# Engine orders as written-out tables in a gated linear attention and squared-relu kernel

## The chip, the cores and the metric

The kernel runs on one core of one Trainium2 chip. The metric is device time in microseconds, from the first to the last instruction of the program; of several runs the median is given.

## The reference

A recurrent linear attention with a decay per channel feeds a two-layer network with a squared relu. 4 batches, 8 heads, 768 tokens, head size 48; the network has width 384 and 2048 hidden units.

```python
def _attn_ref(q, k, v, alpha):
    state = np.zeros((B, H, D, D)); y = np.zeros_like(q)
    for t in range(S):
        state = alpha[:, :, t, :, None] * state + np.einsum('bhd,bhe->bhde', k[:, :, t], v[:, :, t])
        y[:, :, t] = np.einsum('bhd,bhde->bhe', q[:, :, t], state)
    return y

def _moe_ref(x, w_in, w_out):
    h = x @ w_in
    r = np.maximum(h, 0.0)
    g = r * r
    return g @ w_out
```

The attention's output, laid out as 3072 tokens by 384, is x. Inputs and output are float32.

## The kernel before

**Units.** The tokens are cut into 12 units (G = 12) of 256 tokens of one batch, numbered 0 to 11; units 0 to 3 are the first of their batches, 8 to 11 the last. The recurrence is computed in chunks: running sums of the logarithms of alpha give decay factors, with which q and k are scaled, so that the work inside a chunk is matmuls, and a state of 48 x 48 per head is handed from a batch's unit to its next.

**Steps of a unit g, with the names that the text uses** (a name is that of an operation handed to `Program.add`):

- loads: `lda`, `ldk`, `ldq`, `ldv` (L568), four DMAs of 384 KB into RAW, of which there are four buffers. Those of unit 2 go through GpSimd's queue, all others through SyncE's. All loads of a unit from 4 on wait until `ldq` of the unit before has landed; from unit 5 on `lda` also waits for the unit before's `ln`, `ldk` for its `ekm`, `ldq` and `ldv` for its `tr0`. The loads of unit 3 wait for the weight load `wout0`. `win0`, `win1`, `wout0`, `wout1` (L539) bring the two layers' weights in two halves each (768 KB on arrival, as bf16) through GpSimd's queue; `win0` and `win1` wait for `lda1`, and `lda2` to `ldv2`, `wout0` and `wout1` wait for `ldv1`.
- front: `pr` (product of two tokens' alphas, L675 or L677), `ln` (L678) and `lm` (L717) on ScalarE, `m1i` (running sum, a matmul, L684 and L687; units 2 and 3 also have `m1s`), `ei`, `ea`, `ec` (exponentials out of PSUM, L695 to L700), `bk` (L702 or L704), `lb` (L719), `es` (L721; in units 2 and 3 L709, followed by `aq`), then `ekm` (L751) and `eqm0`, `eqm1` (L746), which scale k and q. `vc` casts v to bf16 (L741 on GpSimd or L742 on ScalarE; L613 in unit 0). `tr0` and `tr1` (L762) transpose the scaled q and k by DMA from unit 3 on, before that on TensorE, with `et` as the copies out of PSUM (L641, L783). Unit 0's front is cut by heads, so that its names have one digit more (`ekm0_0`, `ekm1_0`, `tr01_0`).
- attention: `p` (scores, L940), `mk0` and `mk1` (the causal mask, L951), `kv` (keys by values, L811), `sa`, `sc`, `sd` (the state, L904 to L917), `y` (the output, L832 and L843; from y2 to y10 it holds the `kv` of the next unit too), `xe` (copy out of PSUM, L971), `xt` (transpose; on TensorE, L986, with the copy `xv` up to unit 3, by DMA on SyncE's queue, L992, from unit 4 on).
- network: eight steps `s1_g_u` (six matmuls each, L1042) write two PSUM banks in turn; `re` takes the relu (512 columns, L1050 on ScalarE or L1052 on VectorE); `sq` squares it, 1024 columns where u is 1, 3 or 5, and 512 where it is 6 or 7 (L1060 on VectorE, L1064 on ScalarE; the form for GpSimd stands at L1063). Two times four steps `s2_g_j_s` (four matmuls each, L1089) sum into the one bank psO, `oe_g_j` (L1097 or L1099) copies it out, and `out` (L1109) stores 384 KB. The last half tile of unit 11 is cut into two parts of 272 and 112 columns (L1012, L1017, L1019, L1020).

**What sets the order.** Each operation is added with the engines that may run it, a cost for each, a priority, and the keys that it reads and writes. `schedule` (L159) then plays the program through with these costs, with a rate for each DMA and with corrections of the priorities from the table SHIFT, and so gives every operation an engine and a place in that engine's order. `fill` (L271) puts matmuls of zeros (L1143, 512 or 256 columns) on TensorE where it expects idle time ahead of the first s1. `place` (L298) works out which semaphores each operation has to wait for, and `emit` (L348) writes each engine's instructions in that order. On the chip every engine takes its instructions strictly in that order.

TensorE's order around unit 7 and 8 before: `y8 s1_7_2 s1_7_3 m1i10 s2_7_0_0 s1_7_4`. SyncE's: `ldq9 ldv9 out5_1 lda10 ldk10 tr0_9 tr1_9 out6_1 xt8 ldq10 ldv10 lda11`. GpSimd's start: `vc0 win0 win1 sd0 lda2 ldk2 ldq2 ldv2 wout0 wout1 sd1 pr3`.

Of the kernel before, what the change touches and what calls it, by code (L numbers as in the profile page):

```python
# [2 lines left out]

# [28 lines left out]


class Program:

    HOP = 35
    PE_LATENCY = 170
    DMA_FIRST = {"sp": 1300, "act": 1300, "pool": 2000}  # L40
    PACKET = (("win", 172), ("wout", 490), ("ld", 22), ("tr", 18), ("xt", 18), ("out", 125))
    SBUF_ONLY = ("pr", "bk", "aq", "ekm", "eqm", "sq", "sb", "sd")
    BIAS = {"pool": 300}
    DMA_LAST = {"sp": 800, "act": 800, "pool": 1900}
    SWITCH = 95
# [1129 lines left out]
```

## Time and profile before

| | |
|---|---|
| runs | 175.18, 175.5, 174.51 us; median 175.18 |
| the profiled execution's span | 174.5 us |
| granted TensorE clock | 1.000 |
| first s1 matmul, last matmul, last end | 18.46, 171.91, 174.47 us |
| ScalarE: relus L1050 | 83, 596 ns each |
| VectorE: relus L1052 | 13, 687 ns each |
| VectorE: squares L1060 | 30 of 1024 columns, 712 ns; 17 of 512, 424 ns |
| ScalarE: squares L1064 | 6 of 1024 columns, 1057 ns; 7 of 512, 631 ns |
| SyncE's DMAs, 384 KB load, issue to landing | 4.2 to 5.1 us (medians) |
| GpSimd's weight loads, issue to landing | 9.9 and 15.2 us (medians) |

The page is of one execution. An engine's busy time is the union of its instructions; PE is TensorE's matmuls, PEld its weight loads, DVE VectorE, ACT ScalarE, POOL GpSimd, SP SyncE, of which only the queue (SPq) issues. In the strips of 40 digits each stands for a fortieth of the span, in tenths of it busy. A group has the line, the engine, the operation, its output and inputs with shapes, the count, then busy us and mean ns of one, then the idle time just ahead of its instructions and who ended it. A line of a timeline has the start in us, the duration, the engine, and at its end in brackets the idle time before.

### The profile page before, as it was taken

What the parts mean: (1) busy time and instruction counts of PE and PEld (TensorE: products, weight loads), DVE (VectorE), ACT (ScalarE), POOL (GpSimd) and SP (SyncE); (2) the same over time, 40 slices, a digit from 0 to 9 for tenths busy, and PEclk for the clock granted to TensorE, in tenths of its full rate; (3) what the DMA queues carried; (4) which work ended last, traced back from release to release, by engine and by line L of the source; (5) the groups of instructions that cost most, each with busy time, mean ns of one, the idle gap of its engine ahead of it and who ended that gap; (6) DMA issues with size and microseconds to landing.
All of it is one profiled execution on the core that took longest, in us unless ns stands there. A gap on an engine that the chain in (4) does not pass through costs nothing.

```text
span 174.5 us, 5094 instructions
## 1 busy us (share of the span) xinstructions
PE 169.1 (97%) x2237; PEld 130.5 (75%) x2237; DVE 121.3 (70%) x197; ACT 117.6 (67%) x211; POOL 18.8 (11%) x28
## 2 busy tenths in 40 slices
PE   7989999999999999999999999999999999999994
PEld 2556898856886697777788886778788697688773
DVE  5497799797967869866778966868849726322230
ACT  3848698868869569768768757378668564566440
POOL 3159010022102120000100000000200000000000
DMA  5999999979998999798998897999899690040022
GB/s 139 324 297 190 274 303 216 230 208 280 274 229 125 274 235 188 200 222 151 278 212 211 228 196 180 275 201 251 201 214 208 115 196 4 0 135 4 10 80 90
DMA packets 74743, 33.36 MB, mean 191 GB/s; under 512 B 71649, under 2 KB 71905, under 8 KB 74721
## 3 DMA queue, kind: packets, MB, share of 16 engines
q1 hardware_dynamic: 73184, 28.32, 71.4%
q0 software_dynamic: 1536, 4.72, 12.1%
q8 instruction: 17, 0.28, 0.7%
q14 instruction: 6, 0.04, 0.1%
HBM read 25.17 MB, written 4.72 MB: 171 GB/s over the span
## 4 chain that ended last, share of the span: by engine, by line
PE 56%; DMA 26%; ACT 6%; DVE 4%; SPq 3%; POOL 2%; issue 1%
PE psO L1089 22%; PE psWH L1042 22%; DMA raw<-in_v_dram 9%; DMA wout<-in_moe_w_out_dram 8%; DMA raw<-in_alpha_dram 5%; DMA raw<-in_q_dram 5%; SPq L568 3%; PE psO L1143 2%; POOL raw L568 2%; ACT rr L1050 2%; PE psX L843 2%; PE psX L1012 2%; ACT vbf L742 1%; PE psZ L811 1%; PE psX L832 1%; PE psX L940 1%
## 5 line engine op out<-in xcount | busy, mean ns | idle before, releaser
L1042 PE MATMUL psWH<-xt,win 128*128 128x256 bf16 x576 | 73.9, 275 | 0.5 <-ACT rr L1050 0.2
L1042 PEld LDWEIGHTS psWH<-xt,win 128*128 128x128 bf16 x576 | 65.0, 145 | 6.2 <-DVE rr L1052 1.6
L1089 PE MATMUL psO<-wout,gt 128*128 128x384 bf16 x368 | 68.9, 326 | 0.0
L1050 ACT ACTIVATE rr<-psWH 128x512 bf16<-128x512 f32 x83 | 48.9, 596 | 21.5 <-PE psWH L1042 20.0
L1089 PEld LDWEIGHTS psO<-wout,gt 128*128 128x128 bf16 x368 | 34.8, 98 | 18.3 <-DVE gt L1060 0.2
L1060 DVE TENSOR_TENSOR gt<-rr 128x1024 bf16<-128x1024 bf16 (+1 forms) x47 | 28.4, 608 | 25.1 <-ACT rr L1050 24.5
L951 DVE TENSOR_TENSOR pm<-psX,caus 128x1024 bf16<-128x1024 f32 x12 | 14.6, 1220 | 2.4 <-PE psZ L940 2.1
L951 DVE TENSOR_TENSOR pm<-psZ,caus 128x1024 bf16<-128x1024 f32 x12 | 14.6, 1216 | 1.5 <-PE psZ L940 1.4
L1097 ACT ACTIVATE osb<-psO 128x384 f32<-128x384 f32 x19 | 9.3, 489 | 6.8 <-PE psO L1089 6.3
L971 ACT ACTIVATE xbf<-psX 128x768 bf16<-128x768 f32 x12 | 9.7, 806 | 5.0 <-PE psX L832 4.1
L746 DVE TENSOR_TENSOR qks<-raw,eq 128x384 bf16<-128x384 f32 x18 | 10.3, 605 | 3.0 <-DMA raw<-in_q_dram 3.0
L1143 PE MATMUL psO<-zero 128*128 128x512 bf16 (+1 forms) x37 | 10.5, 417 | 1.3 <-DVE zero L489 1.3
L741 POOL CAST vbf<-raw 128x768 bf16<-128x768 f32 x4 | 3.7, 930 | 71.5 <-DMA raw<-in_v_dram 71.5
L1064 ACT ACTIVATE gt<-rr 128x512 bf16<-128x512 bf16 (+1 forms) x13 | 10.8, 828 | 0.4
L751 DVE TENSOR_TENSOR qks<-raw,ek 128x768 bf16<-128x768 f32 x11 | 10.7, 969 | 0.4 <-ACT ek L663 0.3
L1052 DVE TENSOR_SCALAR rr<-psWH 128x512 bf16<-128x512 f32 x13 | 8.9, 687 | 2.0 <-PE psWH L1042 1.6
L742 ACT ACTIVATE vbf<-raw 128x768 bf16<-128x768 f32 x7 | 5.9, 845 | 3.5 <-DMA raw<-in_v_dram 3.5
L717 ACT ACTIVATE la<-raw 128x384 f32<-128x384 f32 x8 | 4.2, 523 | 5.3 <-DMA raw<-in_alpha_dram 5.2
L1143 PEld LDWEIGHTS psO<-zero 128*128 128x128 bf16 x37 | 3.5, 108 | 4.6 <-issue 1.9
L906 DVE TENSOR_TENSOR smd<-psZ,sbd 128x384 bf16<-128x384 f32 x8 | 4.4, 554 | 3.4 <-PE psX L832 3.4
L675 DVE TENSOR_TENSOR prd<-raw 128x384 f32<-128x384 f32 x7 | 4.0, 569 | 2.9 <-DMA raw<-in_alpha_dram 2.9
L678 ACT ACTIVATE lab<-prd 128x384 bf16<-128x384 f32 x10 | 5.2, 520 | 1.1 <-POOL prd L677 0.6
(115 smaller groups left out, 165.9 us busy)
## 6 DMA issues: line engine op xcount, KB each, us to landing
raw<-in_alpha_dram SPq DMA_DIRECT2D x11, 384.0 KB, 4.2
raw<-in_k_dram SPq DMA_DIRECT2D x11, 384.0 KB, 5.1
raw<-in_q_dram SPq DMA_DIRECT2D x11, 384.0 KB, 4.2
raw<-in_v_dram SPq DMA_DIRECT2D x11, 384.0 KB, 4.8
...
wout<-in_moe_w_out_dram POOLq DMA_DIRECT2D x2, 768.0 KB, 15.2
...
```

What stands on the lines that cost most here:

```text
L746: add("dve", lambda e, j=j, dst=dst: e.tensor_tensor(dst, RAW[r][:, 2, :, j, :].rearrange("p (n x) d -> p n x d", x=2), EQ[la][:, j].rearr ...
L751: add("dve", lambda e, a=a, E=E: e.tensor_tensor(QKS[qs][:, a, :, :, 0:D], RAW[r][:, 1 + a].rearrange("p h j d -> p j h d"), E[la][:].rear ...
L951: add("dve", lambda e, hf=hf, psT=psT: e.tensor_tensor(PM[pm][:, hf].rearrange("p r n j t -> p (r n) (j t)"), psT[:, :, :].rearrange("p r ...
L971: add("act", lambda e: e.activation(XBF[x2][:], psX[:, :, 0:HD], AF.Copy), act_ns(2 * HD), p0 + 6100, reads=[("ps", "X", 0), ("ps", "X", 1 ...
L1042: ins = pe.matmul(psH[hb][:, i * T:(i + 1) * T], WIN[:, kk, hidden(fj)], mov, start=(kk == 0), stop=(kk == KT - 1))
L1050: add("act", lambda e, hb=hb, rr=rr: e.activation(rr, psH[hb], AF.Relu), act_ns(512), pu + 600, reads=[("ps", "H", hb)], writes=[("rr", rb ...
L1052: alts={"dve": (lambda e, hb=hb, rr=rr: e.tensor_scalar(rr, psH[hb], 0.0, None, ALU.max), dve_ns(512))})
L1060: add("dve", lambda e, dst=dst, sq=sq: e.tensor_tensor(dst, sq, sq, ALU.mult), 148 + k * 267, pu + 1200, reads=[("rr", rb, h) for h in ran ...
L1064: "act": (lambda e, dst=dst, sq=sq: e.activation(dst, sq, AF.Square), act_ns(k * 512))})
L1089: ins = pe.matmul(psS, GT[gt][:, fj, j, :], WOUT[:, fj, :], start=(fj * parts % FT == 0), stop=((fj + 1) * parts % FT == 0))
L1097: add("act", lambda e, j=j, psS=psS: e.activation(OSB[ob][:, j], psS, AF.Copy), act_ns(DM), ps_ + 700, reads=[keyS], writes=[("osb", ob, j ...
L1143: pr.fill(lambda n: lambda pe: pe.matmul(psO[:, 0:n], ZERO[:, 0:128], ZERO[:, 0:n], skip_group_check=True), ((512, 216, 420), (256, 109, 2 ...
```

## The change

`schedule`, `fill` and SHIFT go. In their place stand one table for each engine, TABLES, with the names of its operations in order (`+512` and `+256` are the matmuls of zeros), and `arrange`, which gives every operation the engine and the place that the tables say. `sequence` puts the operations of all engines into one order that respects what each depends on, which `place` used to take from the planned start times. In `add` a set `shared` notes operations that are ordered only because both read the same PSUM bank; `place` asks for no semaphore between two such on the same engine. The setup operations get names. The operations themselves, their tiles and their data stay as they are.

```diff
     def add(self, ...):
...
-        op = Op(choices, prio + self.SHIFT.get(name, 0), name)
+        op = Op(choices, prio, name)
...
             if k[0] == "ps":
                 for r in self.readers.get(k, ()):
-                    op.deps.setdefault(r, False)
+                    if r not in op.deps:
+                        op.deps[r] = False
+                        op.shared.add(r)
...
             for r in self.readers.get(k, ()):
                 if r is not op:
                     op.deps.setdefault(r, False)
+                    op.shared.discard(r)
...
+    def arrange(self, tables, make, after):
+        named = {o.name: o for o in self.ops}
...
+        for e, text in tables.items():
+            self.order[e] = []
+            for x in text.split():
+                if x[0] == "+":
+                    o = Op({e: (make(int(x[1:])), 0)}, 0, "fill")
...
+                else:
+                    o = named.pop(x)
+                o.eng = e
+                o.fn, o.cost = o.alts[e]
+                o.pos = len(self.order[e])
+                self.order[e].append(o)
...
+    def sequence(self):
+        done, seq = set(), []
+        at = {e: 0 for e in self.order}
+        while len(seq) < len(self.ops):
+            before = len(seq)
+            for e, ops in self.order.items():
+                while at[e] < len(ops) and all(d in done for d in ops[at[e]].deps):
+                    o = ops[at[e]]
+                    done.add(o)
+                    seq.append(o)
+                    at[e] += 1
...
     def place(self):
-        seq = sorted(self.ops, key=lambda o: (o.start, o.idx))
+        seq = self.sequence()
...
-                if d.sem is None and d.eng == o.eng == "pe":
+                if d.sem is None and d.eng == o.eng and (o.eng == "pe" or not raw and d in o.shared):
                     continue
...
-    pr.schedule()
-    pr.fill(lambda n: lambda pe: pe.matmul(psO[:, 0:n], ZERO[:, 0:128], ZERO[:, 0:n], skip_group_check=True),
-            ((512, 216, 420), (256, 109, 250)), min(o.start for o in pr.order["pe"] if o.name.startswith("s1_")), zero, 4600)
+    pr.arrange(TABLES, lambda n: lambda pe: pe.matmul(psO[:, 0:n], ZERO[:, 0:128], ZERO[:, 0:n], skip_group_check=True),
+               zero)
     pr.place()
     pr.emit()
```

The tables:

```diff
+TABLES = {
+    "act": """
+        table ln0_0 ln1_0 xcaus ei0_0 ei1_0 ea0_0 ea1_0 ec0_0 et00_0 ec1_0 ln1 ei1 ea1 xe0 et0_1 ec1 re0_0 xe1
+        sq0_1 ln2 re0_4 re0_6 ei2 ea2 ec2 es2 re1_1 re1_2 sq0_7 et0_2 re1_3 sq1_1 re1_4 sq1_3 re1_5 oe0_0 ln3
+        vc2 ei3 ea3 ec3 vc3 es3 re1_7 oe0_1 re1_6 lm4 xe2 ln4 sq1_7 ei4 ea4 ec4 sq1_6 re2_0 es4 re2_1 oe1_0
+        sq2_1 re2_3 lm5 ln5 ei5 ea5 vc4 re2_6 re2_7 ec5 oe1_1 es5 xe3 xv3 vc5 re3_1 re3_0 lm6 ln6 xe4 ei6 ea6
+        sq3_1 ec6 oe2_1 re3_5 sq3_5 es6 re3_6 re3_7 re4_0 re4_1 vc6 sq4_1 ln7 oe3_0 ei7 ea7 re4_5 lm7 ec7 re4_4
+        es7 re4_7 sq4_5 oe3_1 vc7 sq4_6 ln8 lm8 oe4_0 re5_3 ei8 ea8 es8 sq5_1 re5_5 re5_4 oe4_1 re6_1 re6_3 vc8
+        lm9 ln9 xe7 ei9 re6_2 re6_7 ea9 es9 sq6_5 re6_6 sq6_3 re7_1 sq6_6 ln10 re7_3 ei10 lm10 ea10 re7_2 re7_4
+        es10 oe6_1 re7_6 re7_7 sq7_6 re8_0 ln11 sq8_1 re8_3 ei11 lm11 sq8_3 re8_4 ea11 re8_7 re8_6 es11 re9_1
+        sq8_6 vc11 re9_3 oe8_0 re9_5 re9_2 sq9_5 re9_7 re9_6 sq9_7 sq9_6 oe9_1 re10_4 re10_5 sq10_7 oe10_0
+        re11_2 sq11_1 re11_4 re11_6 oe11_10 oe11_11
+    """,
+    "dve": """
+        zero zlstr zlb0 zlinc zown zqk1 zla0 zident zones zown0 zcaus1 zqk0 zcaus zown1 ekm0_0 ekm1_0 zlb1
+        eqm0_0 zla1 eqm1_0 et10_0 sa0 et01_0 et11_0 mk0_0 mk1_0 ekm1 eqm1 xv0 et1_1 zqk2 sc0 mk1_1 mk0_1 sa1
+        re0_1 re0_2 re0_3 sq0_3 re0_5 xv1 sc1 re0_7 re1_0 ekm2 aq2 eqm2 sq0_5 et1_2 sq0_6 mk1_2 mk0_2 sq1_5 sd1
+        sa2 ekm3 sc2 eqm1_3 aq3 pr4 eqm0_3 sd2 sa3 xv2 bk4 lb4 eqm1_4 ekm4 eqm0_4 re2_2 pr5 re2_4 sc3 re2_5 sd3
+        mk0_3 mk1_3 lb5 sq2_6 sq2_3 ekm5 sq2_7 sa4 eqm0_5 sc4 eqm1_5 oe2_0 mk0_4 mk1_4 pr6 re3_2 sa5 re3_3 sq3_3
+        bk6 re3_4 ekm6 lb6 sc5 eqm1_6 eqm0_6 mk0_5 sd5 mk1_5 re4_3 re4_2 xe5 sa6 sc6 lb7 ekm7 sq4_7 eqm0_7
+        eqm1_7 re4_6 mk1_6 mk0_6 re5_0 pr8 re5_1 xe6 sa7 re5_2 bk8 lb8 sc7 ekm8 eqm1_8 eqm0_8 sq5_3 re5_7 re5_6
+        sq5_6 mk1_7 mk0_7 pr9 oe5_0 re6_0 sa8 re6_5 sq6_1 bk9 ekm9 sq6_7 lb9 re6_4 eqm1_9 oe5_1 eqm0_9 mk0_8
+        pr10 re7_0 mk1_8 sq7_1 bk10 oe6_0 xe8 lb10 sa9 ekm10 sd6 eqm1_10 eqm0_10 re7_5 mk1_9 mk0_9 re8_1 sq7_5
+        sq7_7 xe9 re8_2 oe7_0 sa10 re8_5 sq8_5 bk11 lb11 oe7_1 sd7 ekm11 eqm1_11 eqm0_11 mk1_10 mk0_10 re9_0
+        xe10 sa11 sq9_1 re9_4 oe8_1 sq9_3 mk1_11 mk0_11 re10_1 re10_0 oe9_0 xe11 re10_2 re10_3 re10_6 re10_7
+        re11_0 re11_1 re11_3 oe10_1 re11_5 sq11_5 re11_7 sq11_7 sq11_6 oe11_0
+    """,
+    "pe": """
+        +512 +512 +512 +512 +512 +512 +512 +512 m10_0 m11_0 +512 +512 +512 +256 tr00_0 +512 +512 +512 +256
+        tr10_0 kv0 tr01_0 p0_0 tr11_0 +512 +512 p1_0 m11 +512 +512 +512 +256 y0 +512 +512 +512 +256 +256 tr0_1
+        xt0 +256 tr1_1 +512 +512 +512 +256 p0_1 s1_0_0 s1_0_1 kv1 s1_0_2 y1 s1_0_3 xt1 s1_0_4 s1_0_5 m1i2 s1_0_6
+        s1_0_7 s1_1_0 s1_1_1 m1s2 s1_1_2 s2_0_0_0 tr0_2 s2_0_0_1 s1_1_3 tr1_2 s1_1_4 s1_1_5 p0_2 s2_0_0_2
+        s2_0_0_3 s1_1_6 s1_1_7 m1i3 s2_0_1_0 kv2 s2_0_1_1 m1s3 s2_0_1_2 s2_0_1_3 y2 s2_1_0_0 s2_1_0_1 xt2 m1i4
+        s2_1_0_2 s1_2_0 s1_2_1 s2_1_0_3 s1_2_2 s1_2_3 s2_1_1_0 s1_2_4 s1_2_5 s2_1_1_1 m1i5 p0_3 s1_2_6 s1_2_7
+        s2_1_1_2 s2_1_1_3 y3 s2_2_0_0 s2_2_0_1 xt3 s2_2_0_2 s2_2_0_3 s1_3_1 p0_4 s1_3_0 s2_2_1_0 s2_2_1_1 s1_3_2
+        y4 s1_3_3 m1i6 s2_2_1_2 s2_2_1_3 s1_3_4 s1_3_5 s2_3_0_0 s1_3_6 s1_3_7 s2_3_0_1 p0_5 s1_4_0 s1_4_1
+        s2_3_0_2 s1_4_2 s1_4_3 s2_3_0_3 y5 m1i7 s1_4_5 s1_4_4 s2_3_1_0 s1_4_7 s2_3_1_1 s2_3_1_2 s2_3_1_3 s1_4_6
+        p0_6 s2_4_0_0 s1_5_1 s1_5_0 s2_4_0_1 s2_4_0_2 y6 s2_4_0_3 s1_5_2 s1_5_3 m1i8 s2_4_1_0 s2_4_1_1 s1_5_5
+        s2_4_1_2 s1_5_4 s2_4_1_3 p0_7 s1_5_7 s1_5_6 s2_5_0_0 s1_6_1 s2_5_0_1 s1_6_0 s1_6_3 s2_5_0_2 s2_5_0_3
+        s1_6_5 y7 m1i9 s1_6_2 s2_5_1_0 s1_6_7 s2_5_1_1 s2_5_1_2 s1_6_4 s2_5_1_3 p0_8 s1_6_6 s2_6_0_0 s1_7_1
+        s1_7_0 s2_6_0_1 s2_6_0_2 s1_7_3 m1i10 s2_6_0_3 s1_7_2 y8 s2_6_1_0 s2_6_1_1 s1_7_4 s1_7_5 s2_6_1_2
+        s2_6_1_3 s1_7_6 p0_9 s2_7_0_0 s1_7_7 s1_8_0 s2_7_0_1 s1_8_1 y9 s1_8_2 m1i11 s1_8_3 s2_7_0_2 s2_7_0_3
+        s1_8_4 s1_8_5 s2_7_1_0 s2_7_1_1 s1_8_7 s2_7_1_2 s2_7_1_3 s1_9_1 s1_8_6 s2_8_0_0 s2_8_0_1 s2_8_0_2 p0_10
+        s1_9_3 s1_9_0 s2_8_0_3 s1_9_5 y10 s2_8_1_0 s1_9_2 s2_8_1_1 s2_8_1_2 s1_9_4 s2_8_1_3 s1_9_7 s1_9_6
+        s2_9_0_0 p0_11 s2_9_0_1 s1_10_1 s1_10_0 s2_9_0_2 y11 s2_9_0_3 s1_10_3 s1_10_2 s2_9_1_0 s2_9_1_1 s2_9_1_2
+        s2_9_1_3 s1_10_4 s1_10_5 s2_10_0_0 s1_10_6 s2_10_0_1 s1_10_7 s1_11_0 s2_10_0_2 s1_11_1 s2_10_0_3 s1_11_2
+        s1_11_3 s2_10_1_0 s2_10_1_1 s2_10_1_2 s2_10_1_3 s1_11_5 s1_11_4 s2_11_0_0 s1_11_7 s1_11_6 s2_11_0_1
+        s2_11_0_2 s2_11_0_3 s2_11_1_0 s2_11_1_1
+    """,
+    "pool": """
+        scaus1 slinc slstr scaus vc0 sident win0 lda2 win1 ldk2 wout0 ldq2 vc1 wout1 ldv2 sd0 pr2 bk2 pr3 bk3
+        bk5 sq2_5 sd4 sq3_7 sq3_6 pr7 sq4_3 bk7 sq5_5 sq5_7 vc9 sq7_3 vc10 pr11 sq8_7 sq10_1 sq10_3 sq10_5
+        sq10_6 sq11_3
+    """,
+    "sp": """
+        lda0 ldv0 ldk0 ldq0 lda1 ldq1 ldv1 ldk1 lda3 ldq3 ldv3 ldk3 ldq4 lda4 ldk4 ldv4 out0_1 tr1_3 lda5 tr0_3
+        tr0_4 ldk5 tr1_4 ldq5 ldv5 out1_1 lda6 tr0_5 tr1_5 ldk6 ldq6 xt4 ldv6 lda7 out2_1 tr0_6 ldk7 tr1_6 ldq7
+        ldv7 xt5 lda8 tr0_7 tr1_7 ldk8 ldq8 xt6 ldv8 lda9 out3_1 tr0_8 ldk9 tr1_8 ldq9 out4_1 xt7 lda10 ldk10
+        ldv9 tr0_9 tr1_9 ldq10 ldv10 xt8 out5_1 lda11 out6_1 tr0_10 ldk11 tr1_10 xt9 ldv11 ldq11 tr1_11 out7_1
+        tr0_11 xt10 xt11 out8_1 out10_1 out9_1 out11_0 out11_10 out11_11
+    """,
+}
```

Counted over the tables and over the order that `schedule` gives before: relus on ScalarE 83 and then 55, on VectorE 13 and then 41; squares on VectorE 47 and then 22, on ScalarE 13 and then 25, on GpSimd 0 and then 13; `oe` on ScalarE 20 and then 15; `xe` on VectorE 0 and then 6; `pr` on GpSimd 3 and then 4, `bk` 0 and then 4, `vc` 5 and then 4, `sd` 3 and then 2; matmuls of zeros 37 and then 32.

More of the change, by code (lines that the diff above doesn't have):

```diff
@@ L15 @@
 class Op:
-    __slots__ = ("alts", "eng", "fn", "cost", "prio", "deps", "idx", "lag", "sem", "start", "end", "pos", "name",
-                 "users", "ndeps", "mode", "ready", "land")
+    __slots__ = ("alts", "eng", "fn", "cost", "prio", "deps", "idx", "lag", "sem", "pos", "name", "mode", "shared")
     def __init__(self, alts, prio, name):
@@ L26, in __init__ @@
         self.sem = None
-        self.users = []
         self.pos = None
         self.mode = ("F", "F")
-        self.ready = 0.0
-        self.start = self.end = self.land = None
+        self.shared = set()
 class Program:
[L38 to L45, printed above, removed]
-    HALVED = {"qks": 3, "kqt": 3, "raw": 3, "ek": 3, "eq": 3, "acm": 2, "laf": 2}
-    AFFINITY = 2500
-    SHIFT = {
[55 rows of a table removed]
-    }
+    HALVED = {"qks": 3, "kqt": 3, "raw": 3, "ek": 3, "eq": 3, "acm": 2, "laf": 2}
     def __init__(self, nc):
@@ new lines, in sequence @@
+    def sequence(self):
[9 more added lines that the diff above has]
+                    at[e] += 1
+            assert len(seq) > before, {e: ops[at[e]].name for e, ops in self.order.items() if at[e] < len(ops)}
+        return seq
@@ L322, in place @@
             mine = []
[L323 removed]
+            for d in sorted(want.values(), key=lambda d: -rank[d]):
                 s, p = stream(d), place_of(d)
@@ L351, in emit @@
         stores = {}
-        for o in sorted((o for o in self.ops if o.name.startswith("out")), key=lambda o: o.start):
-            stores.pop(o.sem[0], None)
-            stores[o.sem[0]] = o
+        for o in self.order["sp"]:
+            if o.name.startswith("out"):
+                stores[o.sem[0]] = o
         final = [(self.dma_sems[k], self.value[o]) for k, o in stores.items()]
```

166 lines of the change are left out of this document (21 added, 145 removed), and 55 rows, old and new, of the table SHIFT.

## The prediction

> **What bounds the kernel now.** I read the page's head first, then the groups by form, then TensorE's own timeline step by step, and last SyncE's queue.
>
> ```profile
> PE 169.1 (97%) x2237; PEld 130.5 (75%) x2237; DVE 121.3 (70%) x197; ACT 117.6 (67%) x211; POOL 18.8 (11%) x28
> PE   7989999999999999999999999999999999999994
> DMA  5999999979998999798998897999899690040022
> ```
>
> TensorE is busy from the second slice to the last but one. Busy alone does not say that it is full, so I counted its 2237 matmuls off against the planner's order, which gives each step a start, and compared start-to-start times. A first-layer step (s1, six matmuls) takes 0.655 us at its shortest and 0.655 at the median, a second-layer step (s2, four) 0.650 and 0.650. So from the first s1 step (18.46 us) to the last matmul (171.91) TensorE is full, but for waits that I can list: surplus over the shortest of its kind is 0.40 after s1_1_1 (26.6 us), 0.26 around kv2 and m1i3 (36.3), 0.15 at m1i6, 0.27 before y5 (73.2), 0.14 around s1_4_7, 0.24 around y7 (98.6), 0.41 before s1_7_3 and 0.27 before s1_7_4: 2.14 us in all. The span is 18.46 of head, 153.5 of stream, 2.56 of tail. No order can win more than the 2.1 and something of head and tail.
>
> ```profile
> 115.41 0.88 PE L1042 MATMUL psWH<-xt,win 128*128 128x256 bf16 x6 [0.19 <-ACT rr L1050]
> 114.34 0.53 ACT L717 ACTIVATE la<-raw 128x384 f32<-128x384 f32 x1 [2.42 <-DMA raw<-in_alpha_dram]
> 114.77 0.58 ACT L1050 ACTIVATE rr<-psWH 128x512 bf16<-128x512 f32 x1
> ```
>
> The largest late wait, read from the timelines: ScalarE stands 2.42 us at lm10, whose alpha has not landed; the relu re7_1 stands behind it in the same queue, and TensorE behind the relu. y5 and y7 are the same: they wait for vc6 and vc8, casts of a v that landed late. The waits come from late loads in in-order queues.
>
> ```profile
> 109.39 0.37 SPq L568 DMA_DIRECT2D raw<-in_alpha_dram  x1
> 110.52 5.14 SPq L762 DMA_TRANSPOSE kqt<-qks  x2
> 115.70 1.30 SPq L1109 DMA_DIRECT2D out_dram<-osb  x1
> 117.04 1.25 SPq L992 DMA_TRANSPOSE xt<-xbf  x1
> 118.33 0.58 SPq L568 DMA_DIRECT2D raw<-in_q_dram  x1
> ```
>
> SyncE's timeline shows why they are late: ldq10 could go when tr0_9 landed (116.67), but stands behind a store and xt8 until 118.33, and lda11 waits for ldq10.
>
> **The change, part by part.** Against the order that before's planner writes, the tables move 28 net relus ScalarE to VectorE, 13 squares to GpSimd (8 of 1024 columns, 5 of 512), 12 more net to ScalarE, and 5 net output copies and 6 xe copies to VectorE.
>
> ```profile
> L1050 ACT ACTIVATE rr<-psWH 128x512 bf16<-128x512 f32 x83 | 48.9, 596 | 21.5 <-PE psWH L1042 20.0
> L1060 DVE TENSOR_TENSOR gt<-rr 128x1024 bf16<-128x1024 bf16 x30 | 21.3, 712 | 19.6 <-ACT rr L1050 19.2
> L1052 DVE TENSOR_SCALAR rr<-psWH 128x512 bf16<-128x512 f32 x13 | 8.9, 687 | 2.0 <-PE psWH L1042 1.6
> L1064 ACT ACTIVATE gt<-rr 128x1024 bf16<-128x1024 bf16 x6 | 6.3, 1057 | 0.1
> L677 POOL TENSOR_TENSOR prd<-raw 128x384 f32<-128x384 f32 x3 | 3.0, 1005 | 20.2 <-DMA raw<-in_alpha_dram 20.2
> ```
>
> *Engine loads.* Every moved operation at its row's mean: ScalarE 14.7 us less, VectorE 12.4 more (133.7 of 174.5). Both lie beside TensorE's stream; without that cover VectorE's 12.4 would be the cost. A relu on VectorE is 0.09 us longer; TensorE sees it only where fewer than two steps (1.3 us) lie between the s1 that fills a bank and the s1 that reuses it, as 0.2 + 0.69 fits. I count 0. The same-engine waits between readers of one PSUM bank also go: ei2 ends at 26.83 and ea2 starts at 26.86, where neighbours without such a wait overlap by 0.10, so some 0.13 us at each of about 20 places, on ScalarE, which has 57 us idle: 0.
>
> *Squares on GpSimd.* No row shows one. From below, the cast of 768 columns at 0.82 gives 1.1 us for 1024; from above L677 (two inputs, 1.005 for 384) gives 2.7, and 1.35 for 512. A square has two inputs, so I take 2.7. The tightest use is unit 10. Counting from the start of s1_10_4: re10_5 is done at 2.1, sq10_5 at 2.15 + 2.7 = 4.85, and s2_10_0_2, which needs it, stands after s1_10_4, s1_10_5, s2, s1, s2, s1, s1 = 4.57: +0.3. The lower bound gives 0, and sq11_3 has over 2 us of room. The Trainium skill (GPSIMD Engine Reference, 3.1 Elementwise) puts a two-input operation at about 2.6 cycles of 1.2 GHz an element and advises VectorE for it; by that a square of 1024 is an estimated 2.2 us, and this +0.3 would be 0.
>
> *Head.* Fill matmuls go from 37 to 32 (one cold at 0.427, three at 0.216, one at 0.109: 1.18 us less), and v0 moves up to second on SyncE, so that vc0 casts at about 5.4 instead of 7.93. In before that cast lay over ekm1_0:
>
> ```profile
> 7.08 0.56 DVE L620 TENSOR_TENSOR qks<-raw,eq 128x384 bf16<-128x384 f32 x1
> 7.95 1.21 DVE L620 TENSOR_TENSOR qks<-raw,ek 128x384 bf16<-128x384 f32 x1
> ```
>
> The same form takes 0.56 alone and 1.21 beside the cast, and TensorE then waited 0.6 us for tr01_0. Together 1.8 us could go, but s1_0_0 needs win0, which landed at 17.91 and whose gate (lda1, still fifth on SyncE, landed 9.08) is unmoved. So 18.46 becomes 18.0: -0.45 (bounds -0.5 and 0).
>
> *GpSimd's queue.* lda2 now stands between win0 and win1, ldk2 and wout0 ahead of the rest. Landings there follow one another: win1 3.72 after win0, lda2 1.22 after that. New: win1 at 17.91 + 1.22 + 3.72 = 22.85. s1_0_4 needs it at 18.0 + 4.17 (its distance in before) + 0.335 (xt1, now ahead of it) = 22.5: +0.35 (0 to 1.2, if the gate of lda2 runs late). wout0 comes about 2.8 us sooner (27.6 for 30.41; ldq2 and ldv2 now follow it), and with it the loads of unit 3 that wait for it.
>
> *Stream.* TensorE's work is the same steps. Summing their shortest times ahead of each, the new order asks for m1i5 after 4.2 us less of work, m1i7 4.5, m1i9 5.1, m1i10 5.0, m1i11 5.1, y9 4.4: the front of a unit starts earlier, so a late one is no longer felt at once. Do the loads follow? The two-unit loop of before: m1i9 to the last eqm 4.7 (105.80 to 110.49), tr0_9 landed 6.2, ldq10 4.0, an lda up to 4.9, product, Ln and hops 1.35: 21.1 us against 25.3 of TensorE work for two units (steps from s1_2_0 to s1_10_0, 12.66 a unit). So a chain that starts 2.8 us sooner, with ldq3 second and ldq4 first in their groups and no store between the transposes and ldq9 to ldq11, can gain about 2 us a unit. Walking it with these durations, lda10 lands near 106 and is needed by 108.1 (below); lda11 lands near 120.5 for a need of 121.1. I take the 2.14 us of waits as gone, and 0.3 for new ones of the kind of the last (bounds: none gone, all gone).
>
> *Tail.* s2_11_0_3 waits for sq11_6 as before. out9_1 now stands behind out10_1; both go after oe10_1 and land within about 4.6 us of s2_10_1_3's end (2.3 for one, 164.80 to 167.10), and oe11_0, which rewrites that buffer, is due at 5.5. The last copy on ScalarE is 0.26 by the two PSUM copies (397 ns for 272 columns, 489 for 384) against 0.275. So 0 (-0.1 to +0.3).
>
> Sum: -0.45 + 0.35 + 0.3 - 2.14 + 0.3 = -1.6. The profiled span of 174.5 becomes 172.9; the median of the runs, 175.18, lies 0.7 above it, and I forecast **173.6**.
>
> **Rivals.** *The loads don't run ahead* (slower). Then TensorE stands at m1i10, in order, with no way round. lda10 landed at 114.32, so m1i10 can start at 115.7; 60.7 us of TensorE work stand behind it in the new order where 55.6 did. 174.5 - 0.4 + 5.1 - 0.3 = 178.9, or 179.6 as a median. For: SyncE's ring is in order, and a transpose behind two loads took 5.14 to issue. Against: the 21.1 of the loop. It decides from where lda10 lands later than about 109.8 (break-even); the forecast needs 108.1.
>
> *Waits for waits.* The order is fixed, and each hold-up passes to what stands behind: more queues now depend on GpSimd and on loads asked for sooner. If as much comes back as goes, head and win1 cancel: 175.2. For: lda11 has 0.6 us of room by my walk. Against: most front steps have 2 us and more.
>
> *GpSimd in VectorE's way.* Besides ekm1_0, sq0_3 took 1.36 beside sd1 where 0.69 is usual, and sd2 itself 1.47 for 0.82.
>
> ```profile
> 22.56 1.36 DVE L1060 TENSOR_TENSOR gt<-rr 128x1024 bf16<-128x1024 bf16 x1
> ```
>
> If squares on GpSimd stretch half-way to that factor of 1.8, a wide one takes 3.7 and a narrow one 1.85: sq10_5 is then 1.3 late and sq10_6 0.5 more, 1.5 above what the sum holds: 175.1. The Trainium skill (GPSIMD Engine Reference, 1. Specifications) says that the two engines share SBUF interfaces and contend where VectorE has two SBUF inputs; the rows above agree.
>
> **How the numbers follow.** Forecast 0.55, waits for waits 0.2, GpSimd 0.1, loads 0.15. What a measurement tells from no change is 0.5%, so faster is under 174.3 and slower over 176.06. The forecast's own range is 172.2 (all waits gone, none new) to 174.5; it lies nearly all in faster. Waits for waits spreads about 175.2: mostly same, a quarter slower. GpSimd splits between faster and same. Loads is slower. Faster 0.6, same 0.2, slower 0.2. The range, 172.2 to 177.0, leaves out the loads rival in full force and little else.
>
> **What would show it.** Right: s1_0_0 near 18.0, m1i10 near 109.5 with lda10 landed before 108, TensorE's listed waits gone, GpSimd squares of 2 to 2.7 us. Wrong: a wait of over 1 us before an m1i, a y or an s1 that ended with a load or with a square on GpSimd; TensorE idle at s1_0_4 for more than 1 us; or TensorE steps themselves longer than 0.655 and 0.650 with nobody waiting.

## The result and the profile after

The changed kernel takes 177.25 us (median of 20 executions, 174.80 to 180.29), the kernel before 175.03 beside it (20, 174.51 to 177.31): a ratio of 1.0067, 95% interval 1.004 to 1.0094. It is slower, by 0.7%, and lies above the forecast of 173.6 and just above its range. The ratios leave out executions more than 1.5% above the fastest of their kernel, which here are 9 of the changed kernel's 20 and 1 of before's 20; by the medians of all 20 the ratio is 1.013. The changed kernel's profiled execution took 175.95 us with a span of 174.2.

The head and the groups of the page after:

```profile
span 174.2 us, 5091 instructions
PE 168.1 (97%) x2232; PEld 130.3 (75%) x2232; DVE 131.0 (75%) x211; ACT 98.9 (57%) x181; POOL 42.3 (24%) x44
PE   7999999998989999999999999999999999999994
L939 ACT ACTIVATE rr<-psWH 128x512 bf16<-128x512 f32 x55 | 32.4, 596 | 27.7 <-PE psWH L931 27.4
L941 DVE TENSOR_SCALAR rr<-psWH 128x512 bf16<-128x512 f32 x41 | 27.8, 687 | 11.8 <-PE psWH L931 11.6
L952 POOL TENSOR_TENSOR gt<-rr 128x1024 bf16<-128x1024 bf16 (+1 forms) x13 | 20.9, 1619 | 59.9 <-ACT rr L939 36.1
```

The work moved as the diff says: 28 relus from ScalarE to VectorE, 13 squares to GpSimd. TensorE's strip stays at 9 from slice 13 to the last but one; its two gaps lie early, in slices 10 and 12 of 4.36 us each. The late stalls of before are gone in this profile. ScalarE around lm10, where before it stood 2.42 us for the alpha:

```profile
111.24 0.60 ACT L939 ACTIVATE rr<-psWH 128x512 bf16<-128x512 f32 x1 [0.95 <-PE psWH L931]
112.10 0.53 ACT L606 ACTIVATE la<-raw 128x384 f32<-128x384 f32 x1
```

lm10 now waits for nothing. SyncE's queue shows that the loads did come sooner:

```profile
107.41 5.00 SPq L651 DMA_TRANSPOSE kqt<-qks  x2
113.03 0.37 SPq L457 DMA_DIRECT2D raw<-in_q_dram  x1
```

ldq10 goes as tr0_9 lands (113.0), with no store and no xt8 ahead of it; in before it went at 118.33. In the head, VectorE's timeline has ekm1_0, which GpSimd's cast had stretched to 1.21, back at about half a microsecond; the line holds ekm0_0 and ekm1_0 together:

```profile
6.79 1.03 DVE L509 TENSOR_TENSOR qks<-raw,ek 128x384 bf16<-128x384 f32 x2 [3.74 <-DMA raw<-in_k_dram]
```

What TensorE waits for instead, from its timeline and ScalarE's:

```profile
40.94 1.47 PE L978 MATMUL psO<-wout,gt 128*128 128x384 bf16 x8
43.18 0.51 PE L875 MATMUL psX<-ident,xbf 128*128 128x128 bf16 x6 [0.77 <-ACT xbf L860]
...
50.56 0.24 PE L576 MATMUL psWH<-ones,lab 128*128 128x2 bf16 x4
51.58 0.42 PE L829 MATMUL psX<-kqt 64*64 64x128 bf16 x16 [0.78 <-DVE rr L941]
```

```profile
41.91 0.52 ACT L606 ACTIVATE la<-raw 128x384 f32<-128x384 f32 x1 [1.02 <-DMA raw<-in_alpha_dram]
42.34 0.79 ACT L860 ACTIVATE xbf<-psX 128x768 bf16<-128x768 f32 x1
```

The six transposes of xt2 wait for xe2; xe2 has what it needs, but stands behind lm4 on ScalarE, and lm4 waits for lda4, which landed at 41.88. It is a stall of the kind that before had at lm10, 70 us sooner. Both of its halves are new. In before xe2 stood ahead of lm4, and lm4 found its alpha there:

```profile
41.68 0.81 ACT L971 ACTIVATE xbf<-psX 128x768 bf16<-128x768 f32 x1 [0.64 <-PE psZ L811]
42.39 0.52 ACT L717 ACTIVATE la<-raw 128x384 f32<-128x384 f32 x1
```

And in before lda4 was the first of unit 4's loads on SyncE, issued at 38.23 and landed at 41.84. The tables put lm4 ahead of xe2, and ldq4 ahead of lda4; lda4 now goes 2.2 us sooner and lands no sooner:

```profile
35.62 0.37 SPq L457 DMA_DIRECT2D raw<-in_q_dram  x1
36.03 0.89 SPq L457 DMA_DIRECT2D raw<-in_alpha_dram  x1
```

The second wait is p0_3; the profile names a relu, but tr0_3, which p0_3 needs too, landed only at 51.5.

Counted as in the prediction (start to start, over the shortest of its kind), TensorE's waits between the first s1 and the last matmul are 2.61 us; counted over every step in the same way, before has 2.35. That makes an account of the whole span. In each profile of this table the span is the start of s1_0_0, plus 151.3 of work, plus the waits, plus 2.34 of tail (from the end of the last matmul), to within 0.05 us. By the way the waits are counted the sum has to close as long as the work and the tail are the same in every profile; that they are is what the table shows:

```
                              s1_0_0   waits   span    of the waits
before                         18.46    2.35   174.5   ahead of 58 us 1.2
before's orders as tables (e2) 18.58    2.65   174.9   p0_3 0.83
after                          17.94    2.61   174.2   xt2 0.93, p0_3 0.82
changed kernel again (e1)      18.16    4.51   176.3   xt2 0.93, p0_3 0.82, s1_6_1 1.70
changed kernel, third (e9)     18.16    4.03   175.8   xt2 1.03, p0_3 0.55, s1_6_1 1.44
squares off GpSimd (e5)        18.80    2.40   174.8   xt2 0.94, p0_3 0.71
before, squares on (e8)        18.53    3.97   176.2   s1_4_7 0.76, s2_7_0_1 0.68, s2_10_0_2 0.65
squares off GpSimd again (e10) 18.06    3.19   174.9   xt2 1.24, p0_3 0.69
two squares off (e11)          18.40    5.36   177.4   xt2 2.02, p0_3 0.71, y8 2.23
front mended, sq. off (e12)    18.85    4.06   176.6   m1i4 0.86, y3 0.43, y8 1.73
ldv9 first, squares off (e14)  17.74    3.15   174.5   xt2 1.59, p0_3 0.76
lda4 first, squares off (e17)  17.77    1.46   172.9   p0_3 0.78
lda4 first, squares on (e18)   18.14    3.08   174.9   p0_3 0.28, s1_6_1 1.90
```

So a kernel can differ here in two things, the start and the waits, and the experiments ask which waits belong to which edit. The wait of p0_3 is not the new orders' alone: e2, with before's orders, has it too, and the profile of before has not.

### The profile page after: what moved, and what is told of

Read it like the earlier page. It is cut to its first block, busy times and chain, and to the rows that moved or that the text cites. A ratio compares the mean times of both kernels' runs of the same rounds, so it can differ in the third digit from the quotient of the medians.

```text
span 174.2 us, 5091 instructions
## 1 busy us (share of the span) xinstructions
PE 168.1 (97%) x2232; PEld 130.3 (75%) x2232; DVE 131.0 (75%) x211; ACT 98.9 (57%) x181; POOL 42.3 (24%) x44
## 4 chain that ended last, share of the span: by engine, by line
PE 69%; DMA 23%; SPq 2%; ACT 2%; POOL 1%; DVE 1%; issue 1%
PE psO L978 30%; PE psWH L931 29%; DMA wout<-in_moe_w_out_dram 7%; DMA raw<-in_q_dram 7%; DMA raw<-in_alpha_dram 6%; PE psX L732 2%; DMA raw<-in_v_dram 2%; PE psX L829 2%; SPq L457 2%; PE psX L721 2%; PE psZ L700 2%; PE psX L901 2%; PE psZ L829 1%; POOL raw L457 1%; PE psWH L573 1%; DVE rr L941 1%
## 5 line engine op out<-in xcount | busy, mean ns | idle before, releaser
L939 ACT ACTIVATE rr<-psWH 128x512 bf16<-128x512 f32 x55 | 32.4, 596 | 27.7 <-PE psWH L931 27.4
L941 DVE TENSOR_SCALAR rr<-psWH 128x512 bf16<-128x512 f32 x41 | 27.8, 687 | 11.8 <-PE psWH L931 11.6
L952 POOL TENSOR_TENSOR gt<-rr 128x1024 bf16<-128x1024 bf16 (+1 forms) x13 | 20.9, 1619 | 59.9 <-ACT rr L939 36.1
L953 ACT ACTIVATE gt<-rr 128x1024 bf16<-128x1024 bf16 (+1 forms) x25 | 22.0, 885 | 5.2 <-DVE rr L941 5.1
L840 DVE TENSOR_TENSOR pm<-psZ,caus 128x1024 bf16<-128x1024 f32 x12 | 14.6, 1219 | 3.8 <-PE psZ L829 3.7
L840 DVE TENSOR_TENSOR pm<-psX,caus 128x1024 bf16<-128x1024 f32 x12 | 14.6, 1218 | 1.7 <-PE psZ L829 1.7
L949 DVE TENSOR_TENSOR gt<-rr 128x1024 bf16<-128x1024 bf16 (+1 forms) x22 | 13.3, 611 | 1.2 <-ACT rr L939 0.9
L988 DVE COPY osb<-psO 128x384 f32<-128x384 f32 x10 | 5.6, 556 | 5.9 <-PE psO L978 5.9
L591 POOL TENSOR_TENSOR ek<-ek,raw 128x384 f32<-128x384 f32 x4 | 4.2, 1051 | 21.4 <-ACT ek L584 21.4
L862 DVE CAST xbf<-psX 128x768 bf16<-128x768 f32 x6 | 5.7, 954 | 2.0 <-PE psX L721 2.0
L860 ACT ACTIVATE xbf<-psX 128x768 bf16<-128x768 f32 x6 | 4.8, 808 | 3.9 <-PE psX L768 2.5
L566 POOL TENSOR_TENSOR prd<-raw 128x384 f32<-128x384 f32 x4 | 4.0, 1002 | 11.2 <-DMA raw<-in_alpha_dram 11.2
```

The source lines that it names most:

```text
L840: add("dve", lambda e, hf=hf, psT=psT: e.tensor_tensor(PM[pm][:, hf].rearrange("p r n j t -> p (r n) (j t)"), psT[:, :, :].rearrange("p r ...
L939: add("act", lambda e, hb=hb, rr=rr: e.activation(rr, psH[hb], AF.Relu), act_ns(512), pu + 600, reads=[("ps", "H", hb)], writes=[("rr", rb ...
L941: alts={"dve": (lambda e, hb=hb, rr=rr: e.tensor_scalar(rr, psH[hb], 0.0, None, ALU.max), dve_ns(512))})
L949: add("dve", lambda e, dst=dst, sq=sq: e.tensor_tensor(dst, sq, sq, ALU.mult), 148 + k * 267, pu + 1200, reads=[("rr", rb, h) for h in ran ...
L952: alts={"pool": (lambda e, dst=dst, sq=sq: e.tensor_tensor(dst, sq, sq, ALU.mult), 200 + k * 840), "act": (lambda e, dst=dst, sq=sq: e.act ...
L953: "act": (lambda e, dst=dst, sq=sq: e.activation(dst, sq, AF.Square), act_ns(k * 512))})
```

## Experiments

**e1, the changed kernel once more**, unedited, for a second profile.

> The changed kernel itself once more, for a second profile and more executions. Theory L (loads asked for sooner: TensorE's fixed order stands at steps that wait for a load, and how long differs from execution to execution): ratio 1.005 to 1.015 again, a spread of over 2 us between executions, and a profile whose waits stand before m1i, p, y or xt steps with a late load or DMA transpose behind them. Rival G (squares on GpSimd and the re-dealt engines): waits before s1 and s2 steps, with relus or squares behind them, of much the same size in every execution. Rival N (nothing but noise): 1.000 with before's spread.

178.35 us, 1.0131 (1.0072 to 1.019). The waits of xt2 and p0_3 are there again, and a third stands beside them. VectorE's timeline, GpSimd's and TensorE's:

```profile
93.52 2.73 DVE L635 TENSOR_TENSOR qks<-raw,eq 128x384 bf16<-128x384 f32 x2 [0.91 <-DMA raw<-in_q_dram]
96.17 0.68 DVE L949 TENSOR_TENSOR gt<-rr 128x1024 bf16<-128x1024 bf16 x1
```

```profile
93.84 1.99 POOL L952 TENSOR_TENSOR gt<-rr 128x1024 bf16<-128x1024 bf16 x1 [14.64 <-ACT rr L939]
```

```profile
95.16 0.81 PE L978 MATMUL psO<-wout,gt 128*128 128x384 bf16 x4
97.51 0.88 PE L931 MATMUL psWH<-xt,win 128*128 128x256 bf16 x6 [1.53 <-DVE rr L941]
```

The first line holds two products, eqm1_8 at its usual 0.55 and eqm0_8, which began at 94.00, just after GpSimd's sq5_5, and ended at 96.25, 0.41 after it: 2.25 us for 0.55. Behind it in VectorE's order stand sq5_3 and the relu for which s1_6_1 waits. In the first profile after, ldq8 had landed earlier (92.22 for 93.50), sq5_3 began at 93.19, ahead of sq5_5 at 93.33, and it was GpSimd's square that took longer, 2.30 us; nothing waited.

**e2, e3, e4, which table does it.** e2 has the new `place` with before's orders of all five engines written as tables; e3 gives it the new order of SyncE alone; e4 is the changed kernel with before's order of SyncE.

```diff
 TABLES = {
-    "sp": """ lda0 ldv0 ldk0 ldq0 lda1 ldq1 ...
+    "sp": """ (the order of before, by name)
...
```

> All five engine orders of the kernel before, written as tables, with the changed place() and its dropped same-engine waits. Every theory that puts the loss into the orders: 0.995 to 1.002 against before. If the new waits' placement were the loss: over 1.005.

> Before's orders on TensorE, ScalarE, VectorE and GpSimd, with the new SyncE order alone (ldv0 second, q before a in unit 4, stores later). Theory L: the loads come sooner and nothing asks for them sooner, so before's late-load waits (y5, y7, re7_1: about 1 us) go: 0.990 to 0.998. Rival G: the new SyncE order is not the matter, 0.998 to 1.003. If the new SyncE order is itself at fault (stores and transposes behind loads): over 1.005.

> The new orders on TensorE, ScalarE, VectorE and GpSimd, with before's SyncE order. Theory L: TensorE asks for m1i 4 to 5 us of work sooner and the loads do not come sooner, so 1.015 to 1.03, with single waits of over 1 us at m1i, y or p steps. Rival G: as the changed kernel, 1.003 to 1.010.

e2: 1.0014 (0.9977 to 1.0051), so tables and the dropped semaphores make no difference that shows. e3: 185.01, 1.0453 (1.0383 to 1.0522), the third of its outcomes: under before's engine orders the new SyncE order is itself a loss, with waits of 1.9 us at p0_3, 1.6 at s1_5_0 and 2.0 at y8. e4: 212.46, 1.2034 (1.1966 to 1.2101), with waits of 6.4 us at s1_6_1, 6.3 at s1_7_7 and 2.9 at m1i10. TensorE's waits in e4, in us, times and longest:

```profile
PE psWH L931 <- DVE rr L941: 12.4, 2, 6.3
PE psWH L931 <- DMA xt<-xbf: 5.5, 3, 4.2
PE psWH L573 <- ACT lab L567: 3.5, 2, 2.8
```

SyncE's order and the engines' orders work only together. e4 is what the rival of loads that don't run ahead looks like when it happens, only dearer than I had it: lda10 lands at 128.4, and the account has 34 us over start, work and tail, where I had 5.1 more than before. Part of it is not waiting: right after the two longest waits the granted clock is 0.50 for some 3 to 4 us, and s1 and s2 steps take 1.3 us in place of 0.65.

**e5 and e8, the squares on GpSimd alone**: e5 takes the 13 squares of the changed kernel to ScalarE, e8 puts the same 13 on GpSimd in before's orders.

```diff
-    "pool": ... bk5 sq2_5 sd4 sq3_7 sq3_6 pr7 sq4_3 bk7 sq5_5 sq5_7 vc9 sq7_3 ...
+    "pool": ... bk5 sd4 pr7 bk7 vc9 ...
+    "act":  ... vc4 sq2_5 re2_6 ... oe4_1 sq5_5 sq5_7 re6_1 ...
```

> The changed kernel with its 13 squares on ScalarE at about the same times, where ScalarE stood idle; all else as changed. Theory G' (a VectorE operation with two SBUF inputs that comes while GpSimd runs a square of 1.9 us waits to its end, and the relus behind it with it; whether they meet differs from execution to execution): ratio 0.993 to 1.004, a spread as before's, and no wait of over 1 us at s1_6_1. Theory L (late loads alone, the squares not the matter): 1.007 to 1.015, as the changed kernel.

> Before's orders with the same 13 squares taken to GpSimd and nothing else. Theory G': 1.003 to 1.012, waits where a VectorE operation of two SBUF inputs meets a square. Theory L: 0.998 to 1.003.

e5: 176.81, 1.0048 (1.0007 to 1.0089), between the two theories' ranges; its profile has no wait at s1_6_1. e8: 178.32, 1.011 (1.0055 to 1.0165); behind the head ten VectorE operations were stretched there beside GpSimd's (some of them beside operations that GpSimd has in before too), by 7.3 us in all, and TensorE's waits went from 2.35 to 3.97. One of the ten, with the square beside it:

```profile
117.51 2.14 DVE L593 TENSOR_TENSOR ek<-ek,raw 128x384 f32<-128x384 f32 x1 [0.32 <-ACT ek L584]
```

```profile
117.34 1.89 POOL L952 TENSOR_TENSOR gt<-rr 128x1024 bf16<-128x1024 bf16 x1 [20.13 <-DVE rr L941]
```

bk10 took 2.14 us for 0.56. In before's orders the squares alone are a loss of 1.1%.

**e6 and e7, the front mended by hand**: xe2 ahead of lm4 (as in before), tr0_3 ahead of lda5, m1i3 to m1i5 later, pr5 behind the relus, vc4 and re2_6 a place or two sooner; e6 with the squares on GpSimd, e7 without.

```diff
-    "act": ... re1_6 lm4 xe2 ln4 ...       "sp": ... tr1_3 lda5 tr0_3 tr0_4 ...
+    "act": ... re1_6 xe2 lm4 ln4 ...       "sp": ... tr1_3 tr0_3 lda5 tr0_4 ...
```

> The changed kernel with the squares left on GpSimd and three places mended where both its profiles show a wait: xe2 ahead of lm4, tr0_3 ahead of lda5, m1i3, m1i4 and m1i5 one or two steps later on TensorE. Theory L: the waits before xt2 (0.93), p0_3 (0.82) and m1i3 (0.26 to 0.58) go, 1 to 2 us: 0.999 to 1.006. Theory G': the same gain, but the spread and the single waits of over 1 us stay.

> Both edits. If G' and L each hold a part, the two gains add: 0.985 to 0.997, faster than the kernel before.

Both missed: e6 179.40, 1.0179 (1.0132 to 1.0226), e7 180.66, 1.0245 (1.0199 to 1.029). lda5 landed at 52.28 in e6 and at 52.89 in e7, for 49.01 in the profile after, and TensorE stood for it at m1i5, 1.8 and 3.2 us. In e7:

```profile
55.59 0.34 PE L573 MATMUL psWH<-lab,linc 128*128 128x384 bf16 x1 [2.96 <-ACT lab L567]
```

xt2's wait went and a longer one came: the load was made later to make a transpose sooner.

**e9 to e12, run beside each other.** e9 is the changed kernel, e10 is e5 again, e11 takes only sq5_5 and sq5_7 off GpSimd, e12 is e10 with the front's engine orders mended and SyncE's left alone.

```diff
-    "dve": ... aq3 pr4 eqm0_3 sd2 sa3 xv2 ...     "pe": ... m1i5 p0_3 s1_2_6 ...
+    "dve": ... aq3 eqm0_3 pr4 xv2 sd2 sa3 ...     "pe": ... m1i5 s1_2_6 p0_3 ...
```

> The changed kernel a third time, for the comparison inside one run of four kernels. Both theories: 1.007 to 1.013 of before, as it was measured twice. The theory that VectorE and GpSimd exclude each other expects in the trace at least one VectorE operation with two SBUF inputs stretched by over 0.7 us beside a GpSimd square, and a surplus on VectorE of 1.5 to 3 us in all; the wait of xt2 at 0.9 us and that of p0_3 at 0.7 to 0.8 us are there again.

> All 13 squares from GpSimd to ScalarE once more. Theory 1 (the collisions on VectorE are the loss, the new orders of the front give back what they gain): 0.6 to 1.0% under the changed kernel of this job, that is 1.000 to 1.005 of before. Rival (the two earlier jobs only had different chips, and the squares on GpSimd cost nothing that reaches TensorE): within 0.3% of the changed kernel, 1.007 or more of before.

> Only sq5_5 and sq5_7 from GpSimd to ScalarE, the other 11 stay. Theory 1a (one place decides: the pair eqm0_8 and sq5_5 with the relus behind it): the time of the kernel with all 13 moved, within 0.3%. Theory 1b (every square on GpSimd has its chance to meet a VectorE operation, and what is lost is spread): half of the way at most, over 0.3% above the kernel with all 13 moved.

> The squares off GpSimd, and two new waits of the changed orders mended without touching SyncE's order: xe2 ahead of lm4 on ScalarE, eqm0_3 ahead of pr4 and xv2 right behind it on VectorE, s2_1_0_2 ahead of m1i4 and s1_2_6 ahead of p0_3 on TensorE. Theory (the front's gain is given back at the waits of xt2 and p0_3): xt2's wait falls from 0.94 to under 0.2 us and p0_3's from 0.70 to under 0.3, and the time falls by 0.8 to 1.2 us against the kernel with the squares alone moved: 0.995 to 0.999 of before. Rival (what is not lost there is lost at the next load, m1i5 or y3, since loads and their order set the pace here): the two waits fall, another of 0.5 us or more stands behind them, and the time stays within 0.3% of the kernel with the squares alone moved.

e9 177.87, 1.0078 (1.0039 to 1.0117); e10 178.26, 1.0086 (1.005 to 1.0123); e11 177.64, 1.0079 (1.0038 to 1.012); e12 177.34, 1.0029 (0.9992 to 1.0066). My theory of the squares missed: side by side, taking them off GpSimd gave nothing, though e9's profile has the wait at s1_6_1 (1.44) and e10's has not. The front counted for more: in e12 the waits of xt2 and p0_3 are gone, 0.86 came back at m1i4 and 0.43 at y3, and the ratio is under e10's by 0.006, though short of the 0.995 to 0.999 expected. e11's profile shows one more loss:

```profile
113.02 0.82 PE L930 MATMUL psWH<-xt,win 128*128 128x256 bf16 x6
115.99 0.18 PE L720 MATMUL psX<-sbd,kqt 64*128 64x48 bf16 x1 [2.16 <-POOL vbf L629]
```

```profile
107.21 0.58 SPq L456 DMA_DIRECT2D raw<-in_k_dram  x1
107.83 1.19 SPq L456 DMA_DIRECT2D raw<-in_v_dram  x1
```

y8 waits for vc9, the cast of v that ldv9 brings (landed 115.0). In the new order ldv9 stands behind lda10, which waits until ldq9 has landed: 103.9 in the profile after, 106.8 here. In before ldv9 was issued ahead of lda10. Three of the nine profiles with the changed orders and ldv9 behind lda10 have the wait (e7, e11, e12: 1.6, 2.2, 1.7).

**e13 to e16**: ldv9 ahead of lda10 (e13), with the squares off GpSimd (e14), with the front mended further (e15), with both (e16).

```diff
-    "sp": ... xt7 lda10 ldk10 ldv9 tr0_9 ...
+    "sp": ... xt7 ldv9 lda10 ldk10 tr0_9 ...
```

> The changed kernel with one issue moved: ldv9 ahead of lda10 and ldk10 on SyncE, so that it no longer stands behind lda10's wait for ldq9 to land. Theory (in a part of the executions ldq9 lands 1.5 us later, lda10 and ldv9 with it, vc9 with them, and y8 and the TensorE stream wait 1.6 to 2.2 us for it): no wait of y8 over 0.3 us, vc9 done before 112.5 us, the median 0.3 to 0.6% under the changed kernel's 1.007 to 1.013, that is 1.002 to 1.007 of before, and the slowest executions nearer to the median. Rival (where ldq9 is late, the other loads are late too, and the order behind it costs nothing): 1.007 or more as before.

> The same, and all 13 squares on ScalarE. Theory of the collisions: once the load is out of the way, taking the squares off GpSimd is worth 0.5 to 0.8% against the kernel with the load alone moved (the 1.4 to 1.7 us that TensorE waits at s1_6_1), so 0.998 to 1.001 of before. Rival (what VectorE is spared, ScalarE pays: 13 squares take it some 12 us more): within 0.3% of the kernel with the load alone moved.

> The load moved, and the front mended: xe2 ahead of lm4, eqm0_3 and xv2 ahead of pr4, m1i4 behind s1_2_1, s1_2_6 ahead of p0_3; squares on GpSimd as in the changed kernel. Theory (xt2 and p0_3 cost the new orders about 1.5 us, which is what the front gains): 0.4 to 0.8% under the kernel with the load alone moved, waits in the front (xt2, m1i4, s1_2_0, p0_3, y3) under 0.8 us together. Rival (the front is bound by its loads: the wait moves on): within 0.3%, and 1 us or more of waits before 58 us.

> All three: load moved, front mended, squares on ScalarE. If the three losses are separate and real, they add: 0.990 to 0.997 of before, a span below 173.5 us. If loads set the pace whatever stands behind them, 0.999 to 1.004.

e13 1.0016 (0.9967 to 1.0064), but 1.009 by the medians of all executions (177.33 against 175.72), so what ldv9 is worth stays unresolved. e14 1.0083 (1.0041 to 1.0124), e15 1.0137 (1.0086 to 1.0188), e16 1.0107 (1.0052 to 1.0163): all three above what their theories expected. No profile of the six kernels with ldv9 ahead has a wait at y8, not even e14's, where ldq9 landed late (105.8) and ldv9 all the same at 108.8. The second mend of the front missed: it put ScalarE's sq1_6 behind a later m1i4, and s2_1_0_3 waited 1.68 us for it. In e15 and e16 TensorE also stood at s1_0_4 for win1, 0.76 and 1.27 us (landed 23.43 and 24.66). e14 left a clean reading: all of its 3.15 us of waits lie in front of 52.4 us, 1.59 of them at xt2 and 0.76 at p0_3.

**e17 and e18, the load itself**: lda4 ahead of ldq4, nothing else new, on e14 and on e13.

```diff
-    "sp": ... ldk3 ldq4 lda4 ldk4 ...
+    "sp": ... ldk3 lda4 ldq4 ldk4 ...
```

> The kernel with ldv9 ahead of lda10 and the squares on ScalarE (1.0083 of before, all its waits in front of 52.4 us), with one more issue moved: lda4 ahead of ldq4 on SyncE. ldq4 landed at 39.4 and lda4 at 41.9 to 42.4 us, so lda4 should land near 40, before ScalarE and VectorE come to lm4 and pr4 (40.8). Theory (the front's gain is given back at the landing of lda4: lm4 holds xe2 and with it xt2, pr4 holds eqm0_3 and with it tr1_3, lda5, tr0_3 and p0_3): both waits fall together, from 1.6 and 0.76 us to under 0.4 each, the span by 1.5 to 2 us, to 0.997 to 1.001 of before. Rival (loads set the pace in the front whatever comes first: what lda4 gains another load loses): another wait of 1 us or more before 58 us, 1.005 or more of before.

> The same two loads moved, squares on GpSimd as in the changed kernel. Theory of the collisions: a wait at s1_6_1 of 1.3 to 1.7 us wherever eqm0_8 or sq5_3 starts while sq5_5 runs, so 0.4 to 0.9% above the kernel beside it with the squares on ScalarE. Rival (ScalarE pays as much as VectorE is spared): within 0.3% of it.

e17: 176.12, 1.0027 (0.9984 to 1.0069), span 172.9; e18: 175.23, 0.999 (0.9953 to 1.0026). lda4 landed at 39.4 in e17 and 39.7 in e18. ScalarE's timeline there, and TensorE's:

```profile
40.58 0.52 ACT L606 ACTIVATE la<-raw 128x384 f32<-128x384 f32 x1
41.00 0.81 ACT L860 ACTIVATE xbf<-psX 128x768 bf16<-128x768 f32 x1
```

```profile
40.77 1.48 PE L978 MATMUL psO<-wout,gt 128*128 128x384 bf16 x8
42.08 0.50 PE L875 MATMUL psX<-ident,xbf 128*128 128x128 bf16 x6
```

xt2's wait is gone in both, and no load took its place; p0_3's stayed in e17 (0.78) and fell to 0.28 in e18, so that part of the expectation missed: everything up to tr0_3 moved forward with TensorE. The squares on GpSimd are no dearer than on ScalarE here either, though e18 has the wait at s1_6_1:

```profile
95.92 0.88 PE L931 MATMUL psWH<-xt,win 128*128 128x256 bf16 x6 [1.74 <-DVE rr L941]
```

With two issues moved the changed orders are level with before within the intervals, e18 by the medians of all executions too (1.000; e17 1.005). No version beats before. How much of this is lda4 is not shown by the times: e13 and e14, without it, were not run beside e17 and e18, and by the medians of all executions the step is 1.009 to 1.000 with the squares on GpSimd, but only 1.006 to 1.005 with them off; e12, with neither load moved, has 1.0029 as well. What is shown is that the wait at xt2 goes.

## Why the prediction was wrong

**The step that failed** is in the stream: "I take the 2.14 us of waits as gone, and 0.3 for new ones". The first half held but for m1i3 (0.26, 0.58 and 0.34 in the three profiles of the kernel), the second did not. By the account all waits came to 2.61, 4.51 and 4.03 us in these profiles, a mean of 3.7, where before's orders have 2.35 and 2.65. Against that stands the earlier start, 18.1 for 18.5. The account gives 3.72 - 2.50 - 0.43 = +0.8 us where I had -1.6. The walk followed the loads of units 9 to 11, where before waited, and not those of unit 4; there it had "ldq4 first" among the things that help, and that was the fault. In the 14 profiles with ldq4 first lda4 landed between 41.9 and 43.6, no sooner than in before (41.84); in e17 and e18, with lda4 first, at 39.4 and 39.7. ScalarE is ready for lda4 1.0 us before it lands (1.7 in e14), and xe2 stands behind its first user there, eqm0_3 (and with it tr1_3, lda5 and tr0_3) behind its first user on VectorE. The wait of xt2 needs both, the late load and lm4 ahead of xe2: e17 and e18 change the load and it goes, with nothing in its place; e12 changes the engines' order and it goes too, but 0.86 comes at m1i4 and 0.43 at y3.

Of the rivals, waits for waits had the mechanism: hold-ups passed to what stood behind and came back elsewhere. I priced it at as much coming back as goes (175.2); more came back. For the rival of the loads I read the 5.14 us of the queue's row as one transpose; the row holds two, and tr0_9's own issue took 3.8.

**What held.** s1_0_0 at 17.94 (forecast 18.0); win1 landed at 22.50 (22.85), wout0 at 27.43 (27.6); lda10 at 108.22, some 2 us behind the walk's 106 but about as needed (108.1), and m1i10 without a wait; lda11 at 122.49 (120.5), for 0.16 us of wait at m1i11. s1_0_4 started right behind xt1, so the +0.35 for win1 did not come in this profile. The tail cost nothing. The engine loads lay beside TensorE as costed (summed over instructions, ScalarE has 14.6 us less and VectorE 12.0 more, for 14.7 and 12.4), and s1 and s2 kept their 0.655 and 0.650.

**GpSimd.** The wide square takes 1.90 us and the narrow one 1.04, not 2.7 and 1.35; the +0.3 for sq10_5 did not come. The rival was right that the two engines hold each other up, but priced the square's own stretch; what costs more is VectorE's, where an operation can lose nearly the whole of GpSimd's instruction (1.7 us), and the place was another (s1_6_1, behind sq5_5). In profiles it costs 1.3 to 1.9 us where the two meet. The Trainium skill (SBUF — State Buffer, SBUF: two separate sides) says that the port pair is locked for a whole instruction and the loser blocks, and the trace agrees: eqm0_8 ended 0.41 after sq5_5. But in five comparisons side by side (e6 and e7, e9 and e10, e13 and e14, e15 and e16, e18 and e17) moving the squares to ScalarE lowered the ratio by 0.003 in one and raised it by 0.001 to 0.007 in four; the two intervals overlap each time, and by the medians of all executions the move lowers the time in two and raises it in three. The rival is shown as a wait, and as a loss in before's orders (e8), not as the cause of the slower median.

**The basis.** I put the median 0.7 above the span. Every execution is 1.7 to 1.8 us longer than its span (175.95 for 174.2), so before's profiled execution took some 176.2, over every one of the runs that I had. By the account a median execution of 175.03, with a span of about 173.3, has 173.3 - 18.5 - 151.3 - 2.3 = 1.2 us of waits, an estimate, where the profiled one has 2.35: the 2.14 that I let go came from an execution that had waited longer than most, and a median one had about half as much to win.

**Open.** The account's 0.8 us stands against 1.2 to 2.3 by the three ratios of the changed kernel (0.0067 to 0.0131 of 175 us); the profiles are single executions. With the estimate of 1.2 us for before in place of 2.50 it would be 3.72 - 1.2 - 0.43 = +2.1. Why e10 and e14, whose profiles show no wait behind 52.4 us, have medians near those of their neighbours with the squares on GpSimd was not found: the profiled executions took 176.62 and 176.27 us, where the medians are 178.26 and 176.73. The same holds for e17 (174.61 for a median of 176.12), so what its longer executions wait for is not known. How much of the loss is lda4 and how much ldv9 is not settled, nor is p0_3's part. Moving the relus alone was not tried.
